# A delta-rule attention and two feed-forward layers on one core: stores gathered into one transfer each, three sums in two banks

## The chip, the cores and the metric

The kernel runs on one core of a Trainium2 chip. The core has five engines with queues of their own: TensorE (PE, matrix multiplies, whose weight loads are listed as PEld), VectorE (DVE), ScalarE (ACT), GpSimd (POOL) and SyncE (SP). SP computes nothing here: it issues transfers between the main memory and the on-chip buffer. POOL issues transfers too. The metric is the device time of one launch in microseconds (us). Three runs of the kernel before gave 1179.63, 1183.51 and 1185.29 us; the median is 1183.51 us.

## The reference, cut to what matters

For each of 4 batches and 8 heads, a 48 by 48 state is updated token by token over 768 tokens:

```
y[t]   = q[t] @ state
v_old  = k_n[t] @ state            # k_n is k divided by its length
state += beta[t] * outer(k_n[t], v[t] - v_old)
```

The outputs of all heads, side by side, are 3072 tokens of 384 numbers. Two feed-forward layers follow:

```
h = x @ w_in;  g = max(h, 0) + alpha * min(h, 0);  x1 = g @ w_out     # first layer
h = max(x1 @ w_in2, 0);                            out = (h * h) @ w_out2   # second layer
```

with 2048 hidden features in both. All inputs are 32-bit numbers. The kernel splits each operand into a high and a low part and spends three multiplies on each product.

## The kernel before, in words

**Chunks and steps.** The 768 tokens are cut into 12 chunks of 64, and each chunk into two units s = 0 and 1 (half of the heads each). The first layer runs on the 256 tokens of one chunk at a time, in 16 steps (hidden blocks j = 0 to 15). A step is `emit_h` (nine multiplies of 256 columns into a bank `h`, then `r`, `gh`, `gl` on ACT and DVE) and, three steps later, `emit_acc` (nine multiplies into the three sums m = 0, 1, 2). The second layer runs on pairs of chunks, 512 columns wide.

**Attention.** It runs ahead of the layer that needs it, as events with a due time in steps. The early stage (`early`) of a unit makes masked copies of the keys: transposes on PE (L313) into a bank, read out by ACT as `kf` and `kbdE`; then the products of keys with keys (L335), read out as `pf` and `go` and stored. `inverse` solves a triangular system of two chunks on DVE from `prob` to `inv`. The later steps (`steps`, `both`) use the results; `b_y` makes the outputs `y` of a unit, ACT writes them to a buffer, and SP stores them to the scratch tensor `x1d` of the chunk. `load_x` loads `x1d` as `xf`, `take_x` splits it into `xh` (ACT) and `xl` (DVE), and the first multiply of the chunk's first step needs these.

**Order.** The program pushes events into a heap by due time; each carries a priority, and a scheduler then settles the order of instructions on every engine at build time. On the chip each engine runs its own queue strictly in that order: an instruction that waits holds up all behind it. On SP, each transfer takes one of eight semaphores in turn, so it also waits for the transfer eight places ahead of it to land.

**Buffers that matter here.** `pf` is one buffer (128 x 512 numbers) and has three users: the key products of `gram` (L336), the masked scores of `b_p` (L491) and the outputs of `b_y` (L502). `r1` has three slots; the layer's `r` (L608) and the finished sums (L633) share them. `xf` is one buffer. `raw` in the weight pool is used for the first keys and for weights of the first layer (L561), and then no more. Multiplies write to accumulator banks of 512 columns, of which the program uses eight: two `pa` (attention), two `h`, one `pe`, and `acc0`, `acc1`, `acc2`. In the first layer a sum fills half of its bank (256 columns). The early stage takes `pe` alone from chunk 2 on (L136).

The edits touch `ebank` (L134), `x1d` (L162), `b_y` (L495 to L509), `load_x` (L532), `emit_acc` (L622) and the constant `EOFF` (L74, used in L650), the number of steps by which the early stage runs ahead.

Of the kernel before, what the change touches and what calls it, by code (L numbers as in the profile page):

```python
# [9 lines left out]
F32 = mybir.dt.float32  # L10
# [11 lines left out]
DM, DFF = 384, 2048  # L22
CH = 64
NCH = S // CH
NU = 2 * NCH
NG = 8
TOK = B * CH
KD = DM // 128
NF = DFF // 128
# [41 lines left out]
HURRY = 0  # L71
PACE = 16
LEAD = 22
EOFF = 44  # L74
KB = 2
LK = 7
GAP = 3
CHAIN = 4
EARLY = 3
INV = 15  # L80


@with_exitstack
def kernel(ctx: ExitStack, tc: tile.TileContext, qT, ktok, vtok, beta, w1, w2, alpha, cmask, hmask, eye, ident, out):
# [14 lines left out]
    def new(p, shape, dt, tag, bufs=1):  # L99
        return p.tile(shape, dt, tag=tag, name=tag, bufs=bufs)  # L100
# [27 lines left out]
    def bank(p=128, cols=CH, tag="pa"):  # L128
        t = psum.tile([128, 512], F32, tag=tag, name=tag, bufs=PB[tag])
        return t[0:p, 0:NG * cols].rearrange("p (g i) -> p g i", g=NG)  # L130

    spare = itertools.cycle(("acc0", "acc1", "acc2", "pe"))

    def ebank(c):  # L134

        return "pe" if c > 1 else next(spare)  # L136


    cm = new(const, [128, 2, CH], F16, "cm")
# [19 lines left out]
    kscr = [dram.tile([128, 2, NG, HD], F16, tag=f"kscr{u}", name=f"kscr{u}") for u in range(NU)]  # L159
    fscr = [dram.tile([HD, 2, NG, 128], F16, tag=f"fscr{u}", name=f"fscr{u}") for u in range(NU)]  # L160
    oscr = [dram.tile([64, NG, 32, 2], F16, tag=f"oscr{u}", name=f"oscr{u}") for u in range(NU)]
    x1d = [dram.tile([128, KD, TOK], F32, tag=f"x1d{c}", name=f"x1d{c}") for c in range(NCH)]  # L162
    x2d = [dram.tile([128, KD, 2, TOK], F32, tag=f"x2d{n}", name=f"x2d{n}") for n in range(NCH // 2)]

    def loan(j, p, n, dt=F16):
# [277 lines left out]
    def steps(u, d, t0):  # L443
        c, s = divmod(u, 2)

        def load_f():
            if not c:
                d["kbd"], d["ktb"] = kept[u]
                return
            d["kbd"] = new(stp, [HD, 2, NG, 128], F16, "kbd", 2)  # L450
            G.dma_start(out=d["kbd"], in_=fscr[u])

        def load_k():
            if not c:
# [12 lines left out]
        def b_r():
            r = vs[u]
            if c:
                ps = bank(cols=D)  # L470
                for g in range(NG):
                    mm3(ps[:, g], d["kbd"][:, :, g], shl[s][:, :, g])
                V.scalar_tensor_tensor(out=r, in0=ps, scalar=sc[c]["r"], in1=r, op0=ALU.mult, op1=ALU.add)
            d["r"] = r
            p = first(0, s)
            split(rhls[0][p], r[p], sc[c]["v"][p])

        def put_s():
            if c:
                d["sbd"] = new(stp, [HD, 2, NG, HD], F16, "sbd", 2)  # L480
                spread(d["sbd"], shl[s], fmask, c < SPC)

        def put_u():
            d["ubd"] = new(stp, [128, 2, NG, HD], F16, "ubd")
            spread(d["ubd"], d["u"], tmask, c < SPC)

        def b_p():
            ps = bank()
            for g in range(NG):
                mm3(ps[:, g], d["kbd"][:, :, g], d["qh"][:, :, g])  # L490
            pf, d["p"] = new(stp, [128, NG, CH], F32, "pf"), new(stp, [128, 2, NG, CH], F16, "ph", PH)  # L491
            V.tensor_tensor(out=pf, in0=ps, in1=cm[:, s:s + 1].to_broadcast([128, NG, CH]), op=ALU.mult)
            split(d["p"], pf, 1.0)

        def b_y():  # L495
            ps = bank()
            for g in range(NG):
                if c:
                    mm3w(ps, d["sbd"], d["qh"], g, True, False)
                mm3w(ps, d["ubd"], d["p"], g, c == 0, True)  # L500
            ps = ps[0:HD]
            y = new(stp, [128, NG, CH], F32, "pf")[0:HD].rearrange("p (a b) i -> p a b i", b=2)  # L502
            for b2 in range(2):
                scaled(y[:, :, b2, :], ps[:, 4 * b2:4 * b2 + 4, :], sc[c]["y"][0:HD])
            y = y.rearrange("p a b i -> p a (b i)")
            cols = slice(128 * s, 128 * s + 128)
            nc.sync.dma_start(out=x1d[c][0:HD, :, cols], in_=y[:, 0:3])
            for m in range(KD):
                nc.sync.dma_start(out=x1d[c][HD:128, m, cols], in_=y[32 * m:32 * m + 32, 3])  # L509

        def b_s():
            if c == NCH - 1:
                return
            ps = bank(cols=D)
            for g in range(NG):
                mm3w(ps, d["ktb"], d["u"], g)
            ps = ps[0:HD]
            f = sc[c]["s"][0:HD]
            if c:
                V.scalar_tensor_tensor(out=st[s], in0=ps, scalar=f, in1=st[s], op0=ALU.mult, op1=ALU.add)  # L520
            else:
                scaled(st[s], ps, f)
            split(shl[s], st[s], sc[c + 1]["v"][0:HD])

        e = GAP * s
        for t, f, ahead in ((-3 + e, load_f, 0), (LK + e, load_k, 0), (-1 + e, prep, 0), (0 + e, b_r, CHAIN),
                            (12 + e, b_s, CHAIN), (e + (PT if c else PT0), b_p, PA), (2 + e, put_s, 0), ((12 if c else UT0) + 2.3 * s, put_u, YA), ((13.2 if c else UT0 + 0.6) + 2.3 * s, b_y, YA)):
            at(t0 + (min(t, 9.5 + e) if c == NCH - 1 and f == b_p else t), f, ahead=max(ahead, C0) if c == 0 else ahead + LA * (c == NCH - 1))
# [3 lines left out]
    def load_x(n):  # L532

        if n < NCH:
            xf[n] = [new(moe, [128, KD, TOK], F32, "xf")]
            nc.sync.dma_start(out=xf[n][0], in_=x1d[n])
        else:
            xf[n] = [new(moe, [128, KD, TOK], F32, "xf"), new(w2p[0], [128, KD, TOK], F32, "xf")]
            for h, t in enumerate(xf[n]):
                nc.sync.dma_start(out=t, in_=x2d[n - NCH][:, :, h])  # L540
# [80 lines left out]

    def emit_acc(layer, t, j):  # L622
        wh, wl = (t[1] for t in wt[layer, j])
        gh, gl = gt.pop((layer, t, j))
        p, w = (w2p[0], 2 * TOK) if layer else (moe, TOK)
        for m in range(KD):
            if j == 0:
                acc[m] = psum.tile([128, 512], F32, tag=f"acc{m}", name=f"acc{m}", bufs=1)[:, :w]
            sl = slice(m * 128, m * 128 + 128)
            for n, (a, g) in enumerate(((wh, gh), (wh, gl), (wl, gh))):  # L630
                nc.tensor.matmul(acc[m], lhsT=a[:, sl], rhs=g, start=(j == 0 and n == 0), stop=(j == NF - 1 and n == 2))  # L631
            if j == NF - 1:
                o = new(p, [128, w], F32, "r1", RB if layer else R1)  # L633
                A.copy(out=o, in_=acc[m])  # L634
                nc.sync.dma_start(out=out[m, :, t * w:(t + 1) * w] if layer else x2d[t // 2][:, m, t % 2], in_=o)


    def start(c):
# [149 lines left out]
```

## Time and profile before

| | us |
|---|---|
| median of three runs | 1183.51 |
| the profiled execution, whole | 1186.89 |
| its span, first to last instruction | 1184.9 |
| PE busy | 1068.8 (90% of the span) |
| DVE busy | 740.3 (62%) |
| ACT busy | 734.9 (62%) |
| POOL busy | 130.1 (11%) |
| mean granted PE clock, share of full speed | 0.945 |

The span has three parts. Until about 160 us the weights of the first layer are prepared and the attention of the first chunk runs. From 160 to about 755 us the first layer and the attention run side by side. After that only the second layer runs. An engine's idle time is told with what ended it; a wait of an engine that is off the path costs nothing by itself. PE's clock has two levels, 1.2 and 2.4 GHz, and the share granted in a stretch is a mean over both.

### The profile page before, as it was taken

To read this page: it belongs to the slowest core of one execution; us is meant where nothing else is said; L and a number is where in the kernel's file an instruction comes from. 1 tells how busy PE (TensorE), PEld (TensorE's weight loads), DVE (VectorE), ACT (ScalarE), POOL (GpSimd) and SP (SyncE) were. 2 spreads that over 40 slices of the span, in tenths; PEclk is the share of its full clock that TensorE was granted. 3 is DMA by queue.
4 is the path that set the end of the run, shared out by engine and by line. 5 is a ranking of instruction groups with operands and counts; after the bars stand their busy time and mean duration, and the time that the engine had idled before them with its cause. 6 is when DMAs were issued, how large, how long until landed. Compare 5 with 4: busy or idle time off the path is not lost.

```text
span 1184.9 us, 25561 instructions
## 1 busy us (share of the span) xinstructions
PE 1068.8 (90%) x9952; PEld 952.3 (80%) x9952; DVE 740.3 (62%) x1968; ACT 734.9 (62%) x1583; POOL 130.1 (11%) x230
## 2 busy tenths in 40 slices
PE   3786379799989979998999998999999999999998
PEld 2344379799989978998999998998888888888886
DVE  7798489589759976986788675999712121121211
ACT  7777557767765766666755654676744545454543
POOL 6122111111110111111100100111000000000000
PEclk9898569799989998998999999999999999999999
DMA  8754644744563456335524313443300001010000
GB/s 287 173 168 131 143 129 106 184 103 119 127 159 87 125 130 150 104 114 136 139 78 98 97 40 117 132 121 110 91 27 27 27 1 54 1 54 1 27 1 27
DMA packets 163721, 116.81 MB, mean 99 GB/s; under 512 B 123632, under 2 KB 143984, under 8 KB 163600
## 3 DMA queue, kind: packets, MB, share of 16 engines
q0 software_dynamic: 17728, 73.74, 20.4%
q1 hardware_dynamic: 145872, 41.44, 15.9%
q8 instruction: 78, 1.28, 0.5%
q14 instruction: 43, 0.35, 0.1%
HBM read 75.82 MB, written 39.32 MB: 97 GB/s over the span
## 4 chain that ended last, share of the span: by engine, by line
PE 63%; DMA 11%; issue 10%; ACT 8%; DVE 6%; SPq 2%; POOL 1%; ACTq 0%; POOLq 0%; DVEq 0%
PE h L606 28%; PE acc L631 27%; PE pa L126 3%; PE pa L116 2%; DMA x2d<-r 2%; DMA prob<-gscr 1%; DMA x1d<-pf 1%; ACT kbdE L103 1%; DMA h<-in_w_dram 1%; DMA vr<-in_vtok_dram 1%; PE h L587 1%; DMA gscr<-pf 1%; ACT pf L103 1%; ACT r L103 1%; SPq L509 1%
## 5 line engine op out<-in xcount | busy, mean ns | idle before, releaser
L619 DVE TENSOR_TENSOR gl<-r,gh 128x256 fp32r<-128x256 f32 (+1 forms) x288 | 146.0, 509 | 272.0 <-ACT gh L618 270.5
L606 PE MATMUL h<-xh,h 128*128 128x256 f32 (+1 forms) x864 | 286.4, 333 | 10.0 <-DVE r L613 5.1
L606 PE MATMUL h<-xl,h 128*128 128x256 f32 (+1 forms) x864 | 281.2, 326 | 0.0
L606 PE MATMUL h<-xh,l 128*128 128x256 f32 (+1 forms) x864 | 279.5, 324 | 0.0
L631 PE MATMUL acc<-gl,h 128*128 128x256 f32 (+1 forms) x864 | 272.2, 323 | 0.0
L631 PE MATMUL acc<-gh,l 128*128 128x256 f32 (+1 forms) x864 | 270.5, 320 | 0.0
L631 PE MATMUL acc<-gh,h 128*128 128x256 f32 (+1 forms) x864 | 249.8, 325 | 8.4 <-ACT r L634 6.4
L606 PEld LDWEIGHTS h<-xh,h 128*128 128x128 f32 x864 | 168.8, 196 | 23.1 <-DVE r L613 6.8
L606 PEld LDWEIGHTS h<-xl,h 128*128 128x128 f32 x864 | 168.9, 196 | 11.1
L606 PEld LDWEIGHTS h<-xh,l 128*128 128x128 f32 x864 | 168.5, 195 | 11.4
L631 PEld LDWEIGHTS acc<-gl,h 128*128 128x128 f32 x864 | 165.7, 192 | 11.4
L631 PEld LDWEIGHTS acc<-gh,l 128*128 128x128 f32 x864 | 165.8, 192 | 11.3
L631 PEld LDWEIGHTS acc<-gh,h 128*128 128x128 f32 x864 | 154.6, 192 | 21.3 <-ACT r L634 7.6
L618 ACT CAST gh<-r 128x256 fp32r<-128x256 f32 (+1 forms) x288 | 136.5, 476 | 51.0 <-DVE r L613 43.7
L615 ACT ACTIVATE r<-h 128x512 f32<-128x512 f32 x96 | 57.1, 596 | 145.3 <-PE h L606 140.4
L103 ACT ACTIVATE r<-h,sgn 128x256 f32<-128x256 f32 x192 | 88.9, 472 | 62.5 <-PE h L606 45.7
L613 DVE SCALAR_TENSOR_TENSOR r<-h,bet,r 128x256 f32<-128x256 f32 x192 | 91.0, 478 | 37.4 <-ACT r L103 36.2
L377 DVE TENSOR_TENSOR col<-prob,inv 128x252 f32<-128x252 f32 (+22 forms) x186 | 64.0, 344 | 1.1
L378 DVE TENSOR_TENSOR inv<-inv,col 128x252 f32<-128x252 f32 (+22 forms) x186 | 63.9, 343 | 0.9
L616 ACT ACTIVATE r<-r 128x512 f32<-128x512 f32 x96 | 60.7, 634 | 2.7
L103 ACT ACTIVATE kbdE<-pe,hm 96x512 f16<-96x512 f32 x82 | 51.4, 680 | 0.8 <-DMA fscr<-kbdE 0.8
L116 PEld LDWEIGHTS <-kbd 96*128 96x128 f16 x1104 | 39.8, 102 | 11.4 <-issue 8.7
(170 smaller groups left out, 1535.8 us busy)
## 6 DMA issues: line engine op xcount, KB each, us to landing
raw<-in_w_dram POOLq DMA_DIRECT2D x35, 384.0 KB, 3.4
h<-in_w_dram POOLq DMA_DIRECT2D x29, 384.0 KB, 5.5
kbd<-fscr POOLq DMA_DIRECT2D x22, 384.0 KB, 4.2
ktb<-kscr POOLq DMA_DIRECT2D x22, 384.0 KB, 3.5
kscr<-ktbE POOLq DMA_DIRECT2D x21, 384.0 KB, 3.3
fscr<-kbdE POOLq DMA_DIRECT2D x21, 384.0 KB, 3.8
vr<-in_vtok_dram POOLq DMA_DIRECT2D x24, 192.0 KB, 3.3
qr<-in_qT_dram POOLq DMA_DIRECT2D x24, 192.0 KB, 2.9
```

Source lines behind the costliest of these rows:

```text
L103: A.activation(out=out, in_=in_, func=ACTF.Copy if isinstance(scale, float) else ACTF.Identity, scale=scale)
L116: nc.tensor.matmul(ps, lhsT=w[:, i], rhs=x[:, j], start=start and n == 0, stop=stop and n == 2)
L126: nc.tensor.matmul(ps[0:w.shape[1], g], lhsT=w, rhs=x[:, j, g], start=start and n == 0, stop=stop and n == 2)
L377: V.tensor_tensor(out=t, in0=row, in1=x[:, :, 0:m, j:j + 1].to_broadcast([128, 2, m, n]), op=ALU.mult)
L378: V.tensor_tensor(out=x[:, :, 0:m, j + 1:], in0=x[:, :, 0:m, j + 1:], in1=t, op=ALU.subtract)
L606: nc.tensor.matmul(ps, lhsT=a[:, sl], rhs=x, start=(n == 0), stop=(n == 8))
L613: V.scalar_tensor_tensor(out=g, in0=ps, scalar=bet[:, j:j + 1], in1=g, op0=ALU.mult, op1=ALU.max)
L615: A.activation(out=g, in_=ps, func=ACTF.Relu)
L616: A.activation(out=g, in_=g, func=ACTF.Square)
L618: A.copy(out=gh, in_=g)
L619: (V if layer or j not in GP else G).tensor_tensor(out=gl, in0=g, in1=gh.bitcast(F32), op=ALU.subtract)
L631: nc.tensor.matmul(acc[m], lhsT=a[:, sl], rhs=g, start=(j == 0 and n == 0), stop=(j == NF - 1 and n == 2))
```

## The change

Six edits. (1) The outputs `y` of a unit leave by one transfer instead of four; `x1d` is laid out as 96 rows of four blocks for that. (2) From chunk 1 on `y` is written to `raw` instead of `pf`. (3) `xf` is loaded by two transfers instead of one. (4) The sums m = 0 and m = 1 of the first layer lie side by side in `acc0`, m = 2 in `acc1`. The first multiply of m = 1 no longer clears the bank, and is issued behind the first of m = 0. (5) A chunk's finished sums are copied into one `xf` buffer instead of three `r1` slots, and leave by one transfer instead of three. (6) From chunk 2 on the early stage alternates between `pe` and the freed `acc2`, and its due times are 4 steps earlier (`EOFF`).

```diff
-EOFF = 44
+EOFF = 48
+YR = (0, 1)
...
+    two = itertools.cycle(("pe", "acc2"))
     spare = itertools.cycle(("acc0", "acc1", "acc2", "pe"))
     def ebank(c):
-        return "pe" if c > 1 else next(spare)
+        return next(two if c > 1 else spare)
...
-    x1d = [dram.tile([128, KD, TOK], F32, ...
+    x1d = [dram.tile([HD, KD + 1, TOK], F32, ...
...
-            y = new(stp, [128, NG, CH], F32, "pf")[0:HD].rearrange(...)
+            y = (new(wpool, [128, 2 * DM], F32, "raw")[...] if c and s in YR else new(stp, [128, NG, CH], F32, "pf")[0:HD]).rearrange(...)
...
-            nc.sync.dma_start(out=x1d[c][0:HD, :, cols], in_=y[:, 0:3])
-            for m in range(KD):
-                nc.sync.dma_start(out=x1d[c][HD:128, m, cols], in_=y[32 * m:32 * m + 32, 3])
+            nc.sync.dma_start(out=x1d[c][:, :, cols], in_=y)
...
-            nc.sync.dma_start(out=xf[n][0], in_=x1d[n])
+            nc.sync.dma_start(out=xf[n][0][0:HD], in_=x1d[n][:, 0:KD])
+            nc.sync.dma_start(out=xf[n][0][HD:128], in_=x1d[n][:, KD].rearrange("(m p) i -> p m i", m=KD))
...
             if j == 0:
-                acc[m] = psum.tile([128, 512], F32, tag=f"acc{m}", name=f"acc{m}", bufs=1)[:, :w]
+                n = m if layer else m // 2
+                if layer or m != 1:
+                    whole = psum.tile([128, 512], F32, tag=f"acc{n}", name=f"acc{n}", bufs=1)
+                acc[m] = whole[:, (0 if layer else m % 2 * w):][:, :w]
...
+                with tc.issue_after(head[0].ins) if m == 1 and layer == 0 and j == 0 else nullcontext():
+                    i = nc.tensor.matmul(acc[m], ..., start=(j == 0 and n == 0 and (layer == 1 or m != 1)), ...)
...
+            elif j == NF - 1:
+                if m == 0:
+                    acc["o"] = new(moe, [128, KD, TOK], F32, "xf")
+                A.copy(out=acc["o"][:, m], in_=acc[m])
+        if j == NF - 1 and not layer:
+            nc.sync.dma_start(out=x2d[t // 2][:, :, t % 2], in_=acc.pop("o"))
```

On SP, at the outputs of chunk 5 (`x1d_198`), the kernel before has this order. `prob`, `tscr`, `diag` belong to the triangular system of the next two chunks, and x2, x3 count equal rows.

```order
L351 DMA prob<-gscr_105 64x16x16 x2
L385 DMA tscr_115<-prob 1024x1x64 x2
L385 DMA tscr_116<-prob 1024x1x64 x2
L507 DMA x1d_198<-pf 288x1x128
L509 DMA x1d_198<-pf 32x128 x3
L351 DMA prob<-gscr_105 64x512 x2
L401 DMA diag<-tscr_115 32x8x64 x3
L507 DMA x1d_198<-pf 288x1x128
L509 DMA x1d_198<-pf 32x128 x3
L401 DMA diag<-tscr_115 32x8x64
L536 DMA xf<-x1d_198 128x768
```

The changed kernel has this in the same place:

```order
L509 DMA x1d_198<-raw 384x1x128
L353 DMA prob<-gscr_105 64x16x16 x2
L387 DMA tscr_115<-prob 1024x1x64 x2
L387 DMA tscr_116<-prob 1024x1x64 x2
L353 DMA prob<-gscr_105 64x512 x2
L403 DMA diag<-tscr_115 32x8x64 x2
L509 DMA x1d_198<-raw 384x1x128
L403 DMA diag<-tscr_115 32x8x64 x2
L341 DMA gscr_106<-pf 128x8x32
L536 DMA xf<-x1d_198 96x768
L537 DMA xf<-x1d_198 32x3x256
```

The store of the first unit has moved ahead of the four `tscr` stores, the store of the second has stayed behind them, and eight transfers have become two.

On ACT, at the end of chunk 2 in the first layer, the sums are read out in this order before (`acc_4514`, `acc_4518`, `acc_4522` are m = 0, 1, 2):

```order
L634 COPY r_5633<-acc_4514 128x256
L103 ACTIVATE pf<-pe 64x8x32 x2
L103 ACTIVATE go<-pe 64x256
L634 COPY r_5639<-acc_4518 128x256
L103 ACTIVATE uh_89<-pa 64x384
L618 CAST gh<-r_5588 128x256
L257 ACTIVATE pe,sq<-vr 128x384
L634 COPY r_5645<-acc_4522 128x256
```

In the changed kernel `acc_4580` is `acc0` and holds m = 0 and m = 1, and `acc_4587` is `acc1` with m = 2:

```order
L104 ACTIVATE r_5547<-h,sgn 128x256
L619 CAST gh<-r_5499 128x256
L648 COPY xf<-acc_4580 128x256
L648 COPY xf<-acc_4587 128x256
L619 CAST gh<-r_5547 128x256
L104 ACTIVATE r_5610<-h,sgn 128x256
L648 COPY xf<-acc_4580 128x256
L104 ACTIVATE r_5697<-h,sgn 128x256
```

The copy of m = 1 has moved behind that of m = 2. PE's last three multiplies of m = 1 (L639) stand between the two copies of `acc_4580` and wait for the first of them.

## Rows read from the trace of the kernel before

**Rows 1.** By stretch: span, busy PE, PEld, DVE, ACT, POOL; PEclk, DMA share, GB/s
```profile
0.00:160.00 160.00, 92.98 (x752) 59.23 (x752) 123.23 (x362) 112.03 (x240) 42.91 (x74) 0.82 0.66 177
160.00:450.00 290.00, 264.15 (x3548) 256.89 (x3548) 229.53 (x655) 200.82 (x467) 41.88 (x75) 0.91 0.50 128
450.00:755.00 305.00, 288.87 (x3673) 281.56 (x3672) 235.22 (x643) 191.70 (x458) 31.69 (x58) 0.97 0.41 106
755.00:1185.00 430.00, 422.79 (x1980) 354.58 (x1980) 152.27 (x309) 230.37 (x421) 13.61 (x24) 1.00 0.14 44
```

**Rows 2.** Waits of ACT, 160 to 735 us: us in total, times, longest
```profile
ACT r L103 <- DMA x2d<-r: 14.4, 5, 4.9
ACT pf L103 <- DMA x1d<-pf: 12.1, 6, 4.2
ACT r L634 <- DMA x2d<-r: 11.9, 5, 3.6
```

**Rows 3.** Waits of PE, 160 to 735 us
```profile
PE pe L335 <- ACT kbdE L103: 12.2, 4, 6.8
PE h L606 <- DVE r L613: 5.1, 5, 2.7
...
PE acc L631 <- ACT r L634: 4.4, 6, 1.2
```

**Rows 4.** Timeline of SP, 424 to 452 us: start, us, operation, idle before
```profile
429.49 3.09 SPq L385 DMA_DIRECT2D tscr<-prob  x4
432.63 0.92 SPq L507 DMA_DIRECT2D x1d<-pf  x1
433.59 3.06 SPq L509 DMA_DIRECT2D x1d<-pf  x3
...
440.73 0.60 SPq L507 DMA_DIRECT2D x1d<-pf  x1
441.38 1.53 SPq L509 DMA_DIRECT2D x1d<-pf  x3
```

**Rows 5.** Timelines of ACT and PE in the same stretch
```profile
428.68 0.82 ACT L103 ACTIVATE pf<-pa,sc 96x256 f32<-96x256 f32 x2
...
439.88 0.83 ACT L103 ACTIVATE pf<-pa,sc 96x256 f32<-96x256 f32 x2 [4.17 <-DMA x1d<-pf]
...
441.98 1.26 ACT L103 ACTIVATE kbdE<-pe,hm 96x512 f16<-96x512 f32 x2
...
443.29 1.44 PE L335 MATMUL pe<-kf,kbdE 96*128 96x64 f16 x24 [6.76 <-ACT kbdE L103]
```

**Rows 6.** Timelines of SP and ACT, 140 to 162 us: the first chunk's outputs
```profile
151.91 0.57 SPq L507 DMA_DIRECT2D x1d<-pf  x1
152.53 1.57 SPq L509 DMA_DIRECT2D x1d<-pf  x3
157.17 0.34 SPq L536 DMA_DIRECT2D xf<-x1d  x1
...
160.15 1.02 ACT L549 CAST xh<-xf 128x256 fp32r<-128x256 f32 x3 [5.27 <-DMA xf<-x1d]
```

**Rows 7.** Transfers: count, KB each, median us from issue to landing
```profile
xf<-x1d SPq DMA_DIRECT2D x12, 384.0 KB, 3.2
x2d<-r SPq DMA_DIRECT2D x36, 128.0 KB, 3.5
xf<-x2d SPq DMA_DIRECT2D x12, 384.0 KB, 3.8
...
x1d<-pf SPq DMA_DIRECT2D x24, 144.0 KB, 2.5
...
x1d<-pf SPq DMA_DIRECT2D x72, 16.0 KB, 2.0
```

**Rows 8.** Timeline of PE, two multiplies of 256 columns that follow each other
```profile
304.40 0.28 PE L606 MATMUL h<-xh,h 128*128 128x256 f32 x1
304.52 0.28 PE L606 MATMUL h<-xl,h 128*128 128x256 f32 x1
```

More of the change, by code (lines that the diff above doesn't have):

```diff
@@ L161 @@
     oscr = [dram.tile([64, NG, 32, 2], F16, tag=f"oscr{u}", name=f"oscr{u}") for u in range(NU)]
-    x1d = [dram.tile([128, KD, TOK], F32, tag=f"x1d{c}", name=f"x1d{c}") for c in range(NCH)]
+    x1d = [dram.tile([HD, KD + 1, TOK], F32, tag=f"x1d{c}", name=f"x1d{c}") for c in range(NCH)]
     x2d = [dram.tile([128, KD, 2, TOK], F32, tag=f"x2d{n}", name=f"x2d{n}") for n in range(NCH // 2)]
@@ L501, in b_y @@
             ps = ps[0:HD]
-            y = new(stp, [128, NG, CH], F32, "pf")[0:HD].rearrange("p (a b) i -> p a b i", b=2)
+            y = (new(wpool, [128, 2 * DM], F32, "raw")[0:HD, 0:NG * CH].rearrange("p (g i) -> p g i", g=NG) if c and s in YR else new(stp, [128, NG, CH], F32, "pf")[0:HD]).rearrange("p (a b) i -> p a b i", b=2)
             for b2 in range(2):
@@ L623, in emit_acc @@
         wh, wl = (t[1] for t in wt[layer, j])
+        head = []
         gh, gl = gt.pop((layer, t, j))
@@ L627, in emit_acc @@
             if j == 0:
-                acc[m] = psum.tile([128, 512], F32, tag=f"acc{m}", name=f"acc{m}", bufs=1)[:, :w]
+                n = m if layer else m // 2
+                if layer or m != 1:
+                    whole = psum.tile([128, 512], F32, tag=f"acc{n}", name=f"acc{n}", bufs=1)
+                acc[m] = whole[:, (0 if layer else m % 2 * w):][:, :w]
             sl = slice(m * 128, m * 128 + 128)
             for n, (a, g) in enumerate(((wh, gh), (wh, gl), (wl, gh))):
-                nc.tensor.matmul(acc[m], lhsT=a[:, sl], rhs=g, start=(j == 0 and n == 0), stop=(j == NF - 1 and n == 2))
-            if j == NF - 1:
-                o = new(p, [128, w], F32, "r1", RB if layer else R1)
-                A.copy(out=o, in_=acc[m])
-                nc.sync.dma_start(out=out[m, :, t * w:(t + 1) * w] if layer else x2d[t // 2][:, m, t % 2], in_=o)
+                with tc.issue_after(head[0].ins) if m == 1 and layer == 0 and j == 0 else nullcontext():
+                    i = nc.tensor.matmul(acc[m], lhsT=a[:, sl], rhs=g, start=(j == 0 and n == 0 and (layer == 1 or m != 1)), stop=(j == NF - 1 and n == 2), skip_group_check=layer == 0)
+                head = head or [i]
+            if j == NF - 1 and layer:
+                o = new(p, [128, w], F32, "r1", RB)
+                A.copy(out=o, in_=acc[m])
+                nc.sync.dma_start(out=out[m, :, t * w:(t + 1) * w], in_=o)
+            elif j == NF - 1:
[4 more added lines that the diff above has]
+            nc.sync.dma_start(out=x2d[t // 2][:, :, t % 2], in_=acc.pop("o"))
     def start(c):
```

## The prediction

> **What bounds the kernel now.** I read the busy time by stretch first. From 755 us on PE is busy 422.8 of 430 us at full clock [rows 1]; the change touches nothing there but the handover, so these 430 us stay. Until 160 us PE is busy 93 of 160 us and DVE 123 [rows 1]; the time there is set by latencies and by DVE. In the 595 us between, PE is busy 264.2 + 288.9 = 553 us, so 42 us are idle. The granted clock there is 0.91 and 0.97: set against full speed, 0.09 x 290 + 0.03 x 305 = 35 us are lost to it. It is a mean over the two levels, 1.2 and 2.4 GHz, so PE ran at the lower one for some time. So 77 us is a ceiling for all that can be won in the first layer.
>
> Next the waits of ACT in that stretch. 14.4 + 11.9 = 26.3 us end with the landing of a store of sums (`x2d`), and 12.1 us with a store of outputs (`x1d`) [rows 2]. ACT works in order, so what PE wants from it waits too. In PE's own waits three rows answer: 12.2 us for `kbdE`, 5.1 us for `r` of a step, 4.4 us for the copies of sums [rows 3].
>
> Last, the worst place. SP stores the first unit's outputs of chunk 5 with four transfers from 432.63 to 436.65 us [rows 4]; the three small ones alone take 3.06 us. ACT wants to write the second unit's outputs to the same `pf` and sits until 439.88 us, 4.17 us. Its `kbdE` comes at 441.98, and PE, which wants that, is idle 6.76 us [rows 5]. The reader sees a store that stops TensorE through a queue that has nothing to do with the sum.
>
> **The change part by part.** The sum is made against the profiled execution: 1186.9 us, 2.0 of it outside the span, 3.4 above the median of the runs shown.
>
> *Outputs of the first chunk* (edits 1 and 3; it still uses `pf`). SP issues 0.57 + 1.57 us for the second unit; the last piece lands before 157.17, the load is issued there, and ACT casts at 160.15 after 5.27 us idle [rows 6]. One transfer of 192 KB needs about 0.6 us of issue, and should land somewhat after the 2.5 us of the 144 KB one [rows 7]. So the load is issued near 155.3 instead of 157.2. Two loads in place of one then cost one more issue, 0.34 us or a little more. Taken: -1.5 us; bounds -3 and 0.
>
> *Outputs of later chunks* (edits 1 and 2). `raw` is one buffer too, and the second unit still waits for the first unit's store. What goes is three of four issues, the other users of `pf`, and, in chunk 5, the place behind the `tscr` stores: in the changed order the first store stands ahead of them. On SP 72 small transfers go and 12 loads come. Their issue runs beside other work; the price is in what ACT waits for. The single place in [rows 5] is 6.76 us of PE. Taken for all: -8 us; bounds -12 (all of ACT's 12.1) and 0 (the wait moves to `raw`).
>
> *Sums* (edit 5). The sums no longer take the three `r1` slots, so no `r` waits for a store; ACT's 26.3 us go. PE stood for 5.1 + 4.4 = 9.5 us of it at most [rows 3]. One store per chunk replaces three, and must land before the next `xf` load, which is most of a chunk later. Taken: -9; bounds -9.5 and 0. At the handover to the second layer it is near: the last copy of chunk 10, its store (3.5 us), the load of the second layer's first half (3.8 us) [rows 7] and its cast stand in one chain, and between copy and cast ACT has only about ten instructions, some 5 us at 0.4 to 0.6 us each. Then ACT sits for about 3 us, with layer work queued behind it. Taken: +3; bounds 0 and +8.
>
> *Two banks for the early stage, 4 steps earlier* (edit 6). The `kbdE` row has 12.2 us in 4 waits, of which 6.8 is the place above; 5.4 are left [rows 3]. Those are waits for ACT, and a second bank makes ACT no faster. It lets the second transposes run while ACT reads the first. Taken: -2; bounds -5.4 and +5. Ahead of the first chunk's split, ten more DVE instructions of the triangular system stand in DVE's order. DVE is busy 123 of 160 us there, so most of them fit. Taken: +1; bounds 0 and +5.
>
> *Two sums in one bank* (edit 4). This adds a wait. PE's last three multiplies of m = 1 wait until ACT has copied m = 0, and the next chunk's first multiply on `acc0` waits until ACT has copied m = 1: 24 waits in 12 chunks. Behind each, PE's whole queue stands. PE has 1.3 to 5 us of other multiplies in between by the new order (256 columns counted at 0.12 us, the distance of two starts [rows 8]); before it had 3 to 16. The price of one comes from the nearest row: PE waited 6 times for such a copy, 4.4 us together, 0.73 us each [rows 3]. I take 12 of 24 at 0.73: +9 us. Bounds: 0, and 24 at the longest one of that row, 1.2 us: +29.
>
> The Trainium skill (PSUM — Partial Sum Buffer, "PSUM bank collisions raise a hardware error") says that two engines must not be in the same bank and the same 32-partition quadrant at once, even at different columns, so software has to guard by bank. By that rule the 24 waits cannot be ordered away; without it the term would be 0 and the sum 9 us lower. No row of the kernel before shows two first-layer sums in one bank.
>
> *Clock.* 35 us of clock loss stand beside 42 us of idle. Where idle goes, the drop behind it may go too. Net idle removed in the first layer is 8 + 9 + 2 - 9 - 3 = 7 us; in proportion 35 / 42 x 7 = 6. Taken: -6; bounds -20 and +10.
>
> Sum: -1.5 - 8 - 9 + 3 - 2 + 1 + 9 - 6 = -13.5, that is 1173.4 for an execution like the profiled one, and 1183.5 - 13.5 = 1170 us for a median. Most of my "taken" values for gains lie well inside what the waits hold, and issue time won on SP in the crowded places is in none of them; so I lean two us further and forecast 1168.
>
> **The rivals.**
>
> *The crowded places empty out* (1144 us). For it: the idle of PE is not spread but sits in four or five places where SP is full of `tscr`, `prob`, `diag`, `x1d` and `x2d`; 84 fewer transfers there, an earlier key stage and free ACT could take them all. Then -10 for outputs, -9.5 for sums, -5.4 for `kbdE`, the clock in proportion 35 / 42 x 25 = -21, -1.5 at the start, and +9 for the shared bank: -38, 1145. Against it: nothing in the change touches `prob` or the triangular system, which fill the same places.
>
> *The wait only moves* (1181 us). `raw` is one buffer as `pf` was; the second unit waits for the first one's store, and the `xf` load waits for both. Then outputs and early stage give nothing, the sums' 9 us are paid back by the 9 us of the shared bank, and 1 to 3 us are left from the start and the clock. For it: in chunk 5 the second store still stands behind four `tscr` stores, which took 3.09 us to issue [rows 4].
>
> *The shared bank is the new bound* (1200 us, slower). Each of the 24 waits is as long as the copy's place in ACT's queue. Gains without the clock are 1.5 + 8 + 9 + 2 - 1 - 3 = 16.5 us; 16.5 / 24 = 0.69 us a wait is the point from which nothing is left, and the six waits in [rows 3] were 0.73. At 1.2 us each: +29 - 16.5 = 12.5, and 4 or so of clock behind it: 1200. Against it: the scheduler has set the copies of m = 0 and m = 2 first and put other multiplies between, and two of ACT's main holdups go.
>
> That the change does not do what it says is ruled out for stores and banks by the new order, which has one `x1d` store a unit and key stages in `pe` and `acc2`.
>
> **How the numbers follow.** Forecast 1168 (its own range 1156 to 1177): 0.45. Crowded places empty: 0.20. The wait only moves: 0.15. Shared bank: 0.20. About 0.5%, 5.9 us, is what a measurement of this kernel tells from no change: below 1177.6 is faster, above 1189.4 slower. Faster is the first two, 0.65; same 0.16, with a little of the slower case in it; slower 0.19. For 8 in 10 the range leaves out the lower half of the second case and the upper half of the last: 1143 to 1192.
>
> **What would show it.** In the changed profile ACT's rows "`pf` waits for `x1d`" and "`r` waits for `x2d`" should be gone, with no row "`raw` waits for `x1d`" above 3 us. PE idle between the first chunk's split and 755 us should fall from 42 to about 35, and the clock of that stretch rise above 0.95. The waits of the sums' multiplies (L639) for the copies (L648) should total some 9 us; above 16 the shared bank has taken the gain. The second layer alone should take its 430 us as before. I am wrong in the mechanism if `kbdE` still costs PE 12 us, or if the copies of sums wait for `x2d` in their new buffer.

## The result, and the profile after

The changed kernel takes 1143.69 us (median of four runs, 1142.73 to 1144.73) against 1184.4 us of the kernel before on the same chip: a ratio of 0.9662, 95% interval 0.9631 to 0.9693. It is 41 us faster, where 15.5 were forecast. The time is that of the first rival, "the crowded places empty out" (1144 us), to which 0.20 was given.

By stretch, the rows that answer to [rows 1] (same columns; the second layer now starts at 712 us):

```profile
0.00:160.00 160.00, 99.74 (x752) 62.68 (x752) 128.87 (x372) 111.31 (x241) 42.11 (x74) 0.80 0.66 177
160.00:450.00 290.00, 277.54 (x3948) 271.17 (x3949) 251.15 (x729) 219.10 (x522) 47.84 (x83) 0.98 0.57 142
450.00:712.00 262.00, 253.65 (x3257) 247.92 (x3257) 209.37 (x562) 167.96 (x401) 27.41 (x50) 0.99 0.41 109
712.00:1143.00 431.00, 424.91 (x1999) 356.65 (x1998) 151.19 (x307) 231.37 (x424) 12.37 (x23) 1.00 0.14 44
```

The first 160 us and the second layer (431 us, before 430) take as long as they did. All of the gain lies in the first layer's stretch, 552 us in place of 595. PE is busy 277.54 + 253.65 = 531.2 us there, so it is idle 20.8 us, where it was 42; and its busy time falls by 553.0 - 531.2 = 21.8 us with the same work, since the granted clock is 0.98 and 0.99 in place of 0.91 and 0.97. Half of the gain is idle time, half is clock.

ACT's waits for transfers, 160 to 712 us, which answer to [rows 2]:

```profile
ACT xh L550 <- DMA xf<-x1d: 10.1, 3, 5.4
...
ACT xh L550 <- DMA xf<-x2d: 4.9, 1, 4.9
...
ACT raw L104 <- DMA raw<-in_w_dram: 0.7, 3, 0.4
```

None of the three rows of before is left: ACT waits for no store of outputs or of sums any more. SP still does: its loads of `xf` wait 24.2 us for `x1d` to land, where it was 12.1 before. The first row has the first chunk's wait (5.4 us) in it, the second is the handover to the second layer. PE's waits in the same stretch answer to [rows 3]:

```profile
PE h L607 <- ACT xh L550: 6.4, 3, 4.1
PE acc L639 <- ACT xf L648: 3.8, 1, 3.8
PE pe L315 <- DVE go L111: 2.6, 1, 2.6
```

There is no row for `kbdE` any more. The shared bank shows in one wait of 3.8 us, of 24 that were possible, and that one lies at the handover. ACT sits there for the load of the second layer, its copy of m = 1 stands behind the cast, and PE's next multiply waits for the copy:

```profile
678.40 1.02 ACT L550 CAST xh<-xf 128x256 fp32r<-128x256 f32 x3 [4.92 <-DMA xf<-x2d]
...
679.69 0.36 ACT L648 COPY xf<-acc 128x256 f32<-128x256 f32 x1
...
680.10 0.39 PE L639 MATMUL acc<-gh,h 128*128 128x256 f32 x1 [3.77 <-ACT xf L648]
```

The worst place of before, the outputs of chunk 5 [rows 4, 5], looks like this now. SP first:

```profile
394.98 0.59 SPq L509 DMA_DIRECT2D x1d<-raw  x1
395.82 1.34 SPq L353 DMA_DIRECT2D prob<-gscr  x2
401.01 5.21 SPq L387 DMA_DIRECT2D tscr<-prob  x4
406.31 2.14 SPq L353 DMA_DIRECT2D prob<-gscr  x2
408.55 1.03 SPq L403 DMA_DIRECT2D diag<-tscr  x2
409.62 0.60 SPq L509 DMA_DIRECT2D x1d<-raw  x1
...
413.39 0.31 SPq L536 DMA_DIRECT2D xf<-x1d  x1
```

And ACT:

```profile
394.12 0.83 ACT L104 ACTIVATE raw<-pa,sc 96x256 f32<-96x256 f32 x2 [1.20 <-PE pa L127]
...
404.75 0.83 ACT L104 ACTIVATE raw<-pa,sc 96x256 f32<-96x256 f32 x2
...
416.91 1.02 ACT L550 CAST xh<-xf 128x256 fp32r<-128x256 f32 x3 [2.07 <-DMA xf<-x1d]
```

The first unit's store is issued before the four `tscr` stores, so it has landed by the time the second unit's outputs are written at 404.75: ACT does not wait. PE's longest wait in this place is 2.6 us, for `go` from DVE, where it sat 6.76 us for `kbdE`.

### The profile page after: what moved, and what is told of

The parts are those of the page before. It is cut to its first block, busy times and chain, and to the rows that moved or that the text cites. A ratio compares the mean times of both kernels' runs of the same rounds, so it can differ in the third digit from the quotient of the medians.

```text
span 1142.8 us, 25379 instructions
## 1 busy us (share of the span) xinstructions
PE 1055.8 (92%) x9952; PEld 938.4 (82%) x9952; DVE 740.6 (65%) x1968; ACT 729.7 (64%) x1583; POOL 129.7 (11%) x230
## 4 chain that ended last, share of the span: by engine, by line
PE 66%; issue 12%; DMA 8%; DVE 5%; ACT 4%; POOL 2%; SPq 2%; POOLq 0%; DVEq 0%; ACTq 0%
PE h L607 30%; PE acc L639 29%; PE pa L117 3%; PE pa L127 3%; DMA prob<-gscr 3%; DMA h<-in_w_dram 1%; DMA kscr<-ktbE 1%; DMA vr<-in_vtok_dram 1%; ACT kbdE L104 1%; SPq L353 1%; DMA xf<-x2d 1%; DMA xf<-x1d 1%; DVE inv L380 1%; DMA tscr<-prob 1%; DVE col L379 0%
## 5 line engine op out<-in xcount | busy, mean ns | idle before, releaser
L607 PE MATMUL h<-xh,h 128*128 128x256 f32 (+1 forms) x864 | 282.2, 327 | 8.2 <-ACT xh L550 6.4
L639 PE MATMUL acc<-gl,h 128*128 128x256 f32 (+1 forms) x864 | 275.8, 323 | 0.3 <-DVE gl L620 0.2
L639 PE MATMUL acc<-gh,l 128*128 128x256 f32 (+1 forms) x864 | 273.4, 321 | 0.0
L639 PE MATMUL acc<-gh,h 128*128 128x256 f32 (+1 forms) x864 | 261.0, 324 | 4.0 <-ACT xf L648 3.8
L607 PEld LDWEIGHTS h<-xh,h 128*128 128x128 f32 x864 | 165.4, 192 | 20.9 <-ACT xh L550 6.9
L607 PEld LDWEIGHTS h<-xl,h 128*128 128x128 f32 x864 | 166.0, 192 | 12.7 <-DVE xl L551 1.6
L639 PEld LDWEIGHTS acc<-gl,h 128*128 128x128 f32 x864 | 165.6, 192 | 12.3 <-DVE gl L620 1.1
L607 PEld LDWEIGHTS h<-xh,l 128*128 128x128 f32 x864 | 165.8, 192 | 11.3
L639 PEld LDWEIGHTS acc<-gh,l 128*128 128x128 f32 x864 | 165.7, 192 | 11.3
L639 PEld LDWEIGHTS acc<-gh,h 128*128 128x128 f32 x864 | 159.7, 192 | 15.9 <-ACT xf L648 4.0
L617 ACT ACTIVATE r<-r 128x512 f32<-128x512 f32 x96 | 60.6, 632 | 2.6
L127 PE MATMUL pa<-ph,ubd 128*128 128x64 f16 (+1 forms) x576 | 40.2, 198 | 1.8 <-ACT ubd L104 0.9
```

What stands on the lines that cost most here:

```text
L127: nc.tensor.matmul(ps[0:w.shape[1], g], lhsT=w, rhs=x[:, j, g], start=start and n == 0, stop=stop and n == 2)
L607: nc.tensor.matmul(ps, lhsT=a[:, sl], rhs=x, start=(n == 0), stop=(n == 8))
L617: A.activation(out=g, in_=g, func=ACTF.Square)
L639: i = nc.tensor.matmul(acc[m], lhsT=a[:, sl], rhs=g, start=(j == 0 and n == 0 and (layer == 1 or m != 1)), stop=(j == NF - 1 and n == 2), ...
```

## Where the gain was made

ACT casts `xh` anew for each chunk, and the first of these casts opens the chunk's first step; the distance between the first casts of two chunks is the chunk's period, in us in the table. Chunks come in pairs (0 and 1, 2 and 3, and so on), and the two chunks of a pair wait for one triangular system (`prob`, `tscr`, `diag`). I call the period that ends with the load of a pair's second chunk odd (0-1, 2-3, 4-5, 6-7), and the others even. An odd period has two strands in it: the outputs of the second chunk (`x1d`), with whose load (`xf`) it ends, and the key stage (`kbdE`, `gscr`) and the start of the system of the *next* pair. An even period ends with the load of that next pair's first chunk, whose outputs need the system.

| period | 0-1 | 1-2 | 2-3 | 3-4 | 4-5 | 5-6 | 6-7 | 7-8 |
|---|---|---|---|---|---|---|---|---|
| before | 67.4 | 47.7 | 58.2 | 50.7 | 65.8 | 46.5 | 62.8 | 45.1 |
| after | 53.6 | 47.5 | 49.2 | 50.0 | 56.7 | 50.2 | 53.8 | 46.6 |

The four odd periods lose 14, 9, 9 and 9 us; the even ones grow by 4 us together, and 5 us are won behind chunk 8. So nearly the whole gain is made in four places, and at first sight by the strand of the outputs. SP shows both strands in the first odd period. Before (the chunk starts at 160):

```profile
202.49 3.07 SPq L385 DMA_DIRECT2D tscr<-prob  x4
...
219.31 0.58 SPq L507 DMA_DIRECT2D x1d<-pf  x1
219.93 1.61 SPq L509 DMA_DIRECT2D x1d<-pf  x3
...
223.65 0.34 SPq L536 DMA_DIRECT2D xf<-x1d  x1
```

After (it starts at 160 too):

```profile
190.78 0.59 SPq L509 DMA_DIRECT2D x1d<-raw  x1
191.47 5.30 SPq L387 DMA_DIRECT2D tscr<-prob  x4
...
203.53 0.59 SPq L509 DMA_DIRECT2D x1d<-raw  x1
206.53 0.32 SPq L536 DMA_DIRECT2D xf<-x1d  x1
```

The next pair's `tscr` is stored 11 us earlier, the second unit's outputs 16 us earlier, and the load is issued 17 us earlier. Counted from the opening of the period, the second unit's outputs are earlier in all four odd periods, by 16, 17, 7 and 19 us; `tscr` is so in the first and third alone (32, 52, 41 and 47 us behind the opening, before 42, 38, 45 and 42). Which edit does that, and whether both are needed, the experiments must tell.

## The experiments

The theories in the expectations: S, the stores and their buffers make the gain; B, the second bank and the earlier due times make it; D, the due times are the heart of it; P, several of the edits are needed together. In short: S was refuted, B alone too, and P held in kind but not in number: e12, for which it gave 1162 to 1178 us, took 1186.7. D stays open: e13 is 6.7 us slower than e12, between the 5 and the 10 us that were to decide. e1, e7, e8, e11, e16, e18 and e21 fell outside both of their ranges. The table sums the odd and the even periods of the profiled execution up to chunk 8; a ratio is to the kernel before on the same chip. The runs stand on several chips, whose medians of the kernel before differ by up to 3.6 us, so differences of medians are good to some 4 us.

| label | kernel | median us | ratio, 95% interval | odd | even |
|---|---|---|---|---|---|
| | before | 1182.9 to 1186.5, by chip | 1 | 254 | 190 |
| | after | 1143.69 | 0.966 (0.963 to 0.969) | 213 | 194 |
| e2 | before + edits 1 to 3 | 1180.94 | 0.998 (0.996 to 1.000) | 205 | 232 |
| e3 | before + edit 5 | 1179.93 | 0.998 (0.995 to 1.000) | 260 | 186 |
| e11 | before + 1, 2, 3, 5 | 1187.18 | 1.004 (1.002 to 1.006) | 201 | 241 |
| e12 | before + 4, 6 | 1186.71 | 1.004 (1.002 to 1.006) | 242 | 195 |
| e13 | before + 4, 6 without due times | 1193.45 | 1.009 (1.006 to 1.011) | 223 | 223 |
| e1 | before + due times | 1209.93 | 1.020 (1.011 to 1.028) | 264 | 206 |
| e4 | after, one key bank | 1169.49 | 0.988 (0.985 to 0.991) | 226 | 205 |
| e9 | e4 without the shared bank | 1169.76 | 0.986 (0.982 to 0.990) | 228 | 208 |
| e5 | after, old due times | 1166.18 | 0.984 (0.980 to 0.988) | 211 | 217 |
| e6 | after, outputs in `pf` | 1163.85 | 0.982 (0.978 to 0.985) | 228 | 199 |
| e7 | after without 1 to 3 | 1166.47 | 0.983 (0.981 to 0.985) | 240 | 194 |
| e10 | after without 1 and 3 | 1144.10 | 0.964 (0.963 to 0.966) | 207 | 201 |
| e8 | after without 5 | 1161.62 | 0.980 (0.975 to 0.986) | 210 | 206 |

### The edits alone

**e2_outputs_only**, the outputs by one transfer each from `raw` (the layout of `x1d` and the two loads of `xf`, left out here, as in the change):

```diff
-            y = new(stp, [128, NG, CH], F32, "pf")[0:HD]...
+            y = (new(wpool, [128, 2 * DM], F32, "raw")[...] if c and s in YR else new(stp, ..., "pf")[0:HD])...
...
-            nc.sync.dma_start(out=x1d[c][0:HD, :, cols], in_=y[:, 0:3])
-            for m in range(KD): ...
+            nc.sync.dma_start(out=x1d[c][:, :, cols], in_=y)
```

> The kernel before with edits 1 to 3 alone: outputs written to raw, one store a unit, two loads of xf; sums, banks and due times as before. Theory S (the gain is made by the stores and the buffers they hold): the 6.8 us place and the other waits of pf for x1d go, 12 to 20 us faster than before, 1164 to 1172. Theory B (the gain is made by the second bank of the key stage and its earlier due times): under 6 us, 1178 to 1186, PE still waits about 12 us for kbdE.

**e3_sums_one_store**, the sums copied to one `xf` buffer and stored at once:

```diff
+                if m == 0:
+                    acc["o"] = new(moe, [128, KD, TOK], F32, "xf")
+                A.copy(out=acc["o"][:, m], in_=acc[m])
+        if j == NF - 1 and not layer:
+            nc.sync.dma_start(out=x2d[t // 2][:, :, t % 2], in_=acc.pop("o"))
```

> The kernel before with edit 5 alone: the finished sums copied to one xf buffer and stored by one transfer; three banks of their own. Theory S: the 26 us of ACT waits for x2d go, and the step multiplies no longer stand behind them, 10 to 20 us faster, 1164 to 1174. Theory B: under 6 us, 1178 to 1186.

**e11_stores_only**, both of these:

```diff
+            nc.sync.dma_start(out=x1d[c][:, :, cols], in_=y)
...
+            nc.sync.dma_start(out=x2d[t // 2][:, :, t % 2], in_=acc.pop("o"))
```

> The kernel before with edits 1, 2, 3 and 5: all the stores of the change, but three banks for the sums, one bank for the key stage and the old due times. Theory S: most of the 41 us, 1146 to 1158. Theory B: 10 us at most, 1174 to 1184, so that 30 us are left to the banks and the due times.

All three are at the time before to within 0.4%, so the stores alone are worth nothing. The table says why, and it is not that they do nothing: in e2 and e11 the odd periods shrink by 49 and 53 us, more than in the changed kernel. The even periods grow by 42 and 51. SP of e2, in the period from 314 to 375 us (chunk 3 to 4):

```profile
328.12 2.97 SPq L386 DMA_DIRECT2D tscr<-prob  x4
...
362.15 6.46 SPq L508 DMA_DIRECT2D x1d<-raw  x2
371.11 0.32 SPq L535 DMA_DIRECT2D xf<-x1d  x1
```

The same period of the changed kernel runs from 310 to 360 us:

```profile
313.11 3.57 SPq L387 DMA_DIRECT2D tscr<-prob  x4
...
348.13 6.22 SPq L509 DMA_DIRECT2D x1d<-raw  x2
356.62 0.32 SPq L536 DMA_DIRECT2D xf<-x1d  x1
```

From `tscr` to the outputs of the pair's first chunk it takes 34 us in e2 and 35 in the changed kernel. With the stores alone the system's `tscr` goes out 14 us into the period, in the changed kernel 3. The time won in an odd period is lost to the system of the next pair, which was not started any earlier; in the kernel before, the long odd period had covered for that.

**e1_eoff48**, the due times alone:

```diff
-EOFF = 44
+EOFF = 48
```

> The kernel before with the earlier due times alone (EOFF 48). If the lead of the attention is worth something only once no store holds ACT up: 1176 to 1192, no better than before, with ACT still waiting some 35 us for x1d and x2d. If the lead is worth its 22 us by itself: 1158 to 1166.

**e12_banks_and_due**, edits 4 and 6:

```diff
-EOFF = 44
+EOFF = 48
...
+    two = itertools.cycle(("pe", "acc2"))
...
-        return "pe" if c > 1 else next(spare)
+        return next(two if c > 1 else spare)
...
+                n = m if layer else m // 2
```

> The kernel before with edits 4 and 6 alone: shared bank for the sums, two banks for the key stage, due times 4 steps earlier; outputs and sums stored as before. The four runs so far say that the stores alone gain nothing (1187 us) and that the second key bank is worth 26 us inside the change. Theory B alone (banks and due times are enough, stores are beside the point): 1144 to 1156. Theory P (a pair: the key stage in two banks needs pf and SP free of outputs, the stores need the attention to be early): 1162 to 1178, with ACT waits of pf for x1d and of r for x2d still there.

**e13_banks_only**, the same without the due times:

```diff
 # e12_banks_and_due
-EOFF = 48
+EOFF = 44
```

> As e12, but with the old due times (EOFF 44): edit 4 and the two banks alone. Theory B with the bank as its heart: within 5 us of e12. Theory D (the due times are the heart: a second bank only pays when the key stage may start earlier): 10 us or more slower than e12.

Alone these cost 0.4 to 2.0%; the due times by themselves (e1) make the kernel before 25 us slower. In e12 the other strand stays late. SP of e12 in the first odd period (160 to 227 us):

```profile
188.66 3.81 SPq L387 DMA_DIRECT2D tscr<-prob  x4
...
211.07 0.60 SPq L509 DMA_DIRECT2D x1d<-pf  x1
211.72 1.53 SPq L511 DMA_DIRECT2D x1d<-pf  x3
216.80 0.59 SPq L509 DMA_DIRECT2D x1d<-pf  x1
...
222.66 0.53 SPq L538 DMA_DIRECT2D xf<-x1d  x1
```

`tscr` goes out 14 us earlier than before, the second unit's outputs only 2.5 us earlier. They are written to `pf`, one buffer that the key stage (`gscr<-pf`) and both units share. ACT's waits in e12, 160 to 712 us:

```profile
ACT pf L104 <- DMA x1d<-pf: 18.2, 10, 4.0
ACT r L644 <- DMA x2d<-r: 11.7, 8, 3.0
```

The row that gave edits 1 and 2 their price, 12.1 us before [rows 2], has grown to 18.2. The eight periods of e12 are still 8 us shorter in sum than before; 7 us are lost again behind chunk 8.

### One edit taken out of the changed kernel

**e4_one_early_bank**, the early stage in `pe` alone:

```diff
-    two = itertools.cycle(("pe", "acc2"))
+    two = itertools.cycle(("pe",))
```

> The changed kernel with the key stage in pe alone from chunk 2 on, acc2 idle in the first layer; due times, stores and the shared bank as in the change. Theory S: 0 to 6 us slower than the change, 1144 to 1150. Theory B: 20 to 30 us slower than the change, 1164 to 1174, with PE waiting for kbdE again.

**e9_own_banks**, e11 with the due times; it differs from e4 only in that each of the three sums has its own bank:

```diff
 # e11_stores_only
-EOFF = 44
+EOFF = 48
```

> The kernel before with edits 1, 2, 3, 5 and the earlier due times: three banks for the sums, one bank for the key stage. It differs from e4 by the shared bank alone, and from e11 by the due times alone. If the shared bank costs what was forecast (9 us), it is 9 us faster than e4, 1160; if the wait is hidden, 1166 to 1173. If the due times make the 18 us between e11 and e4, it is at 1165 to 1172 and not at 1187.

**e5_eoff44**:

```diff
-EOFF = 48
+EOFF = 44
```

> The changed kernel with the old due times (EOFF 44). Theory B: 0 to 6 us slower than the change, 1144 to 1150. Theory D: 10 us or more slower, 1154 to 1170, with PE waiting again for the split of x.

**e6_outputs_in_pf**, outputs by one transfer each, but from `pf`:

```diff
-YR = (0, 1)
+YR = ()
```

> The changed kernel with the outputs in pf again, by one store a unit (edit 2 undone, 1 and 3 kept). If the worth of the store edits lies in the buffer (pf held by a store while the key stage and the scores want it): 15 us or more slower than the change, 1159 to 1180, with rows of pf waiting for x1d. If it lies in the number of transfers on SP: 1144 to 1150.

**e7_old_outputs**, edits 1 to 3 undone:

```diff
-            nc.sync.dma_start(out=x1d[c][:, :, cols], in_=y)
+            nc.sync.dma_start(out=x1d[c][0:HD, :, cols], in_=y[:, 0:3])
+            for m in range(KD):
+                nc.sync.dma_start(out=x1d[c][HD:128, m, cols], in_=y[32 * m:32 * m + 32, 3])
... and `y` in `pf`, `xf` by one load
```

> The changed kernel with edits 1 to 3 undone: outputs in pf by four stores, one load of xf; sums in xf by one store. Without outputs and sums as changed it took 1187 (e12). If the outputs make that loss: 1170 to 1187. If the sums make it: 1144 to 1155.

**e10_raw_four_stores**, edits 1 and 3 undone, so four transfers a unit, but from `raw`:

```diff
 # e7_old_outputs
-            y = new(stp, [128, NG, CH], F32, "pf")[0:HD]...
+            y = (new(wpool, [128, 2 * DM], F32, "raw")[...] if c and s in YR else ...)...
```

> The changed kernel with four stores a unit from raw and one load of xf (edits 1 and 3 undone, 2 kept). If the number of transfers on SP matters: 10 us or more slower, 1154 to 1175, with raw waiting for x1d and xh for xf. If only the buffer matters: 1144 to 1150.

**e8_sums_in_r1**, edit 5 undone:

```diff
-                    acc["o"] = new(moe, [128, KD, TOK], F32, "xf")
...
+                o = new(p, [128, w], F32, "r1", RB if layer else R1)
+                A.copy(out=o, in_=acc[m])
+                nc.sync.dma_start(out=... x2d[t // 2][:, m, t % 2], in_=o)
```

> The changed kernel with edit 5 undone: finished sums in the three r1 slots, three stores a chunk, but in the shared bank. If the sums make the loss of e12: 1165 to 1187, with r waiting for x2d by 20 us or more. If the outputs make it: 1144 to 1155.

Each of four things is worth 18 to 26 us here, by medians (the four runs of e8 alone spread from 1155 to 1170 us): the second key bank 1169.5 - 1143.7 = 26, the due times 22.5, the outputs' buffer 20, the sums' buffer 18. They add up to 86, twice the gain: the loss of one already costs half. The table shows the strand that each holds up. Without the outputs' buffer the odd periods grow by 15 (e6), without the due times the even ones by 23 (e5), without the second bank both (e4), without the sums' buffer the even ones by 12 (e8). With half of the change taken out nothing is left: the stores without edits 4 and 6 (e11) take 1187 us, edits 4 and 6 without the stores (e12) take 1187, both together 1144.

The start of the system goes with the length of the even periods in all of these kernels. The table gives, for each even period, how many us behind its opening (a minus: ahead of it) SP stores the first `tscr`, and how long the period is:

| label | 1-2 | 3-4 | 5-6 | 7-8 |
|---|---|---|---|---|
| after | -22: 47.5 | 3: 50.0 | -16: 50.2 | -7: 46.6 |
| e2 | -12: 48.1 | 14: 60.7 | 14: 64.8 | 10: 58.8 |
| e11 | -12: 46.6 | 16: 62.1 | 15: 63.9 | 15: 68.6 |
| e5 | -6: 47.8 | 11: 60.6 | -2: 48.9 | 8: 59.7 |
| e4 | -32: 49.9 | 5: 55.7 | -27: 47.9 | 3: 51.8 |

A `tscr` ahead of the opening stands with 47 to 50 us here (43 to 55 over all runs), one that is 8 to 16 us behind it with 59 to 69. On PE this stands in the row of waits for `xh`: 14.2 us in e4, against 6.4 in the changed kernel and 4.7 before. That e4 would make PE wait for `kbdE` again did not come true (1.4 us in 2 waits). In e8 `tscr` goes out 4 to 21 us ahead of every even period, and these are 48 to 55 us long all the same: what makes the loss there is not shown.

Two things are worth nothing. e10 has the 72 small transfers back (66 of them from `raw`) and is as fast as the changed kernel: it was the buffer, not the number of transfers. The Trainium skill (DMA: Bandwidth & Descriptors, "Rules for kernel authors") advises to coalesce many small transfers into one large; here that shows no gain (1143.69 us with it, 1144.10 in e10). And e9 and e4 differ by 0.3 us: whether two sums share a bank or not made no difference that the runs can tell (those of e9 spread from 1162 to 1173 us). The Trainium skill (PSUM — Partial Sum Buffer, "PSUM bank collisions raise a hardware error") asks software to guard by bank. In the changed kernel the multiplies of other tiles cover that guard everywhere but for the 3.8 us at the handover.

### The due times further

If the due times were a lead that one can add to, 52 should win more. First **e16_eoff52**, and **e18_one_bank_eoff52** to see whether lead makes up for the missing bank.

```diff
-EOFF = 48
+EOFF = 52
```

> The changed kernel with due times 4 steps earlier still (EOFF 52). If lead is still short in the change: 5 to 15 us faster, 1129 to 1139. If 48 steps are enough and more only brings work forward into the crowded first 160 us: 1143 to 1155.

```diff
 # e4_one_early_bank
-EOFF = 48
+EOFF = 52
```

> The changed kernel with the key stage in pe alone and due times of 52 steps. If bank and due times are two ways to the same lead: the 4 steps win back most of the 26 us that the bank was worth, 1146 to 1156. If the bank shortens the key stage itself, whenever it starts: 1164 to 1174 as with 48 steps.

They took 1189.54 us (ratio 1.004, 1.001 to 1.007) and 1205.94 us (1.016, 1.010 to 1.022): 46 us slower than with 48, and 36 slower. The lead theory fell. SP of e16 in the first odd period, now 161 to 239 us:

```profile
192.09 3.86 SPq L387 DMA_DIRECT2D tscr<-prob  x4
...
198.84 0.59 SPq L509 DMA_DIRECT2D x1d<-raw  x1
...
219.00 0.38 SPq L341 DMA_DIRECT2D gscr<-pf  x1
...
225.42 0.38 SPq L341 DMA_DIRECT2D gscr<-pf  x1
...
230.76 0.59 SPq L509 DMA_DIRECT2D x1d<-raw  x1
...
234.37 0.34 SPq L536 DMA_DIRECT2D xf<-x1d  x1
```

In this period `tscr` is no earlier than in the changed kernel (191.47); in the later ones it is, but the even periods hardly gain by it (191 us against 194). And 32 us lie between the two outputs' stores here, where 13 did. ACT of e16 shows what stands between:

```profile
219.79 1.25 ACT L104 ACTIVATE kbdE<-acc,hm 96x512 f16<-96x512 f32 x2
...
221.92 1.26 ACT L104 ACTIVATE kbdE<-pe,hm 96x512 f16<-96x512 f32 x2
...
228.36 0.83 ACT L104 ACTIVATE raw<-pa,sc 96x256 f32<-96x256 f32 x2
```

The next pair's key stage comes ahead of this chunk's second outputs on an engine that works in order. That gave theory O (the loss is this overtaking: it can be counted in the order of the program) against M (each step beyond 48 costs engine time). Three more values, each with that line alone changed, were to tell:

**e20_eoff50**

```diff
-EOFF = 48
+EOFF = 50
```

> The changed kernel with EOFF 50. Theory O: 71 foreign transfers stand between outputs and load in this order (18, 20, 10, 20 in chunks 1, 3, 5, 7), as many as at 52: as slow as there, 1180 to 1195 us. Theory M (loss grows with each step): half way between 48 and 52, 1160 to 1170 us.

**e17_eoff56**

```diff
-EOFF = 48
+EOFF = 56
```

> The changed kernel with due times 8 steps earlier still (EOFF 56). Theory O (the loss at 52 comes from the place of the early work: at 52, work of the next pair stands on SP and ACT between the two output stores of a chunk, 12 + 14 + 16 + 20 foreign transfers in chunks 1, 3, 5, 7, so the load of those chunks is late): in this program's order only 8 foreign transfers stand between the first output store of a chunk and its load, so it comes back to 1140 to 1165 us. Theory M (each step earlier than 48 costs more, because early work takes engine time from what is due): 1200 us or more.

**e21_eoff47**

```diff
-EOFF = 48
+EOFF = 47
```

> The changed kernel with EOFF 47. Theory O: 13 foreign transfers (the changed kernel has 35, with EOFF 44 20): as fast as 48 or faster, 1135 to 1147 us. A gain that grows with the lead up to 48 says 1147 to 1152 us (22.5 us over 4 steps, 5.6 us a step).

| `EOFF` | 44 | 47 | 48 | 50 | 52 | 56 |
|---|---|---|---|---|---|---|
| the changed kernel, us | 1166.2 | 1157.0 | 1143.7 | 1164.1 | 1189.5 | 1162.8 |
| odd, even periods, us | 211, 217 | 211, 204 | 213, 194 | 235, 192 | 263, 191 | 224, 189 |

At 56 the time comes back (1162.8, which O allowed and M did not), at 50 it is half way (1164.1, as M said and O did not), at 47 it is 13 us slower than at 48, and its four runs spread from 1150 to 1167 us. Neither theory holds as it was put. The periods are those of one profiled execution each; that of 47 is the fastest of its four. At 44 two of the even periods are long, where the system comes late. At 50 and 52 the odd ones are, and the overtaking of O is there: 24 to 26 us and 32 to 35 us lie between the two output stores of chunks 1, 3, 5 and 7, where the changed kernel has 9 to 15. What failed in O is the count of transfers as a measure of the time, which is about the same at 50 and at 52. At 56 these gaps are down to 5 to 7 us. There the key stage's `gscr<-pf` stands between the two output stores of chunk 0 instead (150.22 and 162.30), and the first layer opens at 170.1 us in place of 159.9: 10 of the 19 us that 56 loses against 48. What makes the rest, and the 13 us at 47, stays open. None of these was faster than the changed kernel; e10 is as fast.

## Why the prediction was wrong, step by step

*The reading of the kernel before.* Right: the second layer and the start did not move, all the gain lay in the first layer. Of the 77 us that were the ceiling 43 were won: 21.2 us of idle and 21.8 us of PE's busy time. The 77 were somewhat too many, as the 35 us of clock in them count idle time at the lower level too; measured in the same way, the clock's loss is 8.4 us now.

*First chunk's outputs, -1.5.* About nothing. The load is issued 1.2 us earlier (155.98, before 157.17), but ACT casts at 159.88 in place of 160.15 [rows 6]: from the first issue to the cast it takes 3.9 us with two loads, 3.0 with one.

*Later outputs, -8.* In company 20 (e6), alone nothing (e2). The working put the gain on fewer issues, other users of `pf` and the place on SP; e10 shows that the first of these is worth nothing.

*Sums, -9, handover +3.* In company 18 (e8), alone nothing (e3). The handover was sized well: ACT waits 4.9 us for `xf<-x2d`, and PE 3.8 us behind it.

*Two banks -2, due times +1.* **This is the step that failed.** Measured at 26 (e4) and 22.5 (e5). The prediction priced the bank by PE's waits for `kbdE` [rows 3] and the due times by DVE's load before the first chunk. Their work is elsewhere: they set when the triangular system begins, and with it when the next outputs can be had. No row of PE's waits in the kernel before says that, because the long odd periods cover for it; PE has multiplies of the running chunk to fill the time, and only where these run out does it wait, for `xh` (14.2 us in e4). The sentence against the first rival, "nothing in the change touches `prob` or the triangular system", was wrong for the same reason: against the stores alone (e2), `tscr` goes out 10 to 29 us earlier, counted from the opening of the even periods.

*Shared bank, +9.* Mis-sized: 3.8 us in one place, which are the handover's, and nothing that the runs can tell between e9 and e4. The prediction counted 1.3 to 5 us of other multiplies ahead of each wait and still charged half of the 24; in the trace they cover all but that one.

*Clock, -6.* Mis-sized: PE's busy time fell by 21.8 us. The proportion was not far off, as 35 / 42 of the 21.2 us of idle that went would be 17.7; it was fed with 7 us of idle.

*The sum.* Also its form failed. Terms were added as if each edit had its own price. Alone, the parts of the change move the time from 0.2% faster to 2.0% slower; the four in company are worth 18 to 26 us each. The first rival named the right time with the wrong terms: it charged 9 us for the bank and 5.4 us for `kbdE` at most, and gave the rest to stores that alone move nothing.

*What would show it.* ACT's rows for `x1d` and `x2d` are gone, none stands for `raw` behind `x1d`, the clock is above 0.95, the second layer took its 430 us: all as said. PE's idle went to 21, not to 35, and L639's waits to 3.8, not 9. Neither sign of a wrong mechanism came, and the time is 24 us from the forecast all the same: the signs watched the waits that the edits take away, and none of them the periods.

What is not shown: why the edits 1 to 3 shorten the odd periods by more alone (e2) than in company, and what the sums' buffer does in e8. Each edit taken out changes the order on all engines, so the 18 to 26 us are prices of an edit with the order that the scheduler then makes, not of a buffer or bank as such. Neighbouring due times alone move the changed kernel by 13 to 46 us. Whether the kernel before, with some other due times, would come near 1144 us was not tried beyond 48.

## What to carry to other kernels

Where a kernel repeats, measure the period of each repeat and find the strands that can end it, before pricing edits by the waits of the busiest engine: those show where it hurts, not which strand is late. Shorten one strand and the next takes its place, so an edit alone proves little either way; take each out of the whole as well. And where due times feed a scheduler that works greedily, run a few neighbouring values before believing what any one edit is worth.

## What was not expected of the hardware

The clock gave back as much as the idle time did: 21.8 us of PE's busy time beside 21.2 us of idle. With PE idle 42 of 595 us the granted clock was 0.91 and 0.97; with 20.8 of 552 us it was 0.98 and 0.99. In e11, whose time is that of before, it was 0.97 up to 450 us, where PE's idle was 18 us, and 0.93 after, where it was 24 us in 262:

```profile
160.00:450.00 290.00, 272.46 (x3674) 266.29 (x3675) 238.23 (x678) 208.22 (x492) 41.58 (x74) 0.97 0.50 129
450.00:712.00 262.00, 237.93 (x3276) 232.69 (x3275) 200.28 (x551) 163.38 (x382) 27.78 (x50) 0.93 0.40 103
```

One place of the changed kernel shows the two together. Behind the wait of 3.77 us at 680.10 the same multiplies take 0.41 us in place of 0.28, and their starts are 0.21 us apart in place of 0.12, up to about 683.5 us. The granted clock is 1.00 from 668 to 676 us, 0.57 from 680 to 684, and 1.00 again from 684 to 690:

```profile
681.13 0.41 PE L639 MATMUL acc<-gh,l 128*128 128x256 f32 x1
...
684.21 0.28 PE L607 MATMUL h<-xh,l 128*128 128x256 f32 x1
```

Not every wait is followed by that: behind the 2.62 us at 412.09 the granted clock stays at 1.00 (412 to 420 us).
